# A cached-attention decode block: weight loads with longer rows, and part of the output projection and modulation moved to another place

## The chip, the cores and the metric

The kernel runs on one core of one Trainium2 chip. The metric is the device time of one execution in microseconds (us), lower is better. The kernel before takes 687.1 us (median of 3 runs, 687.01 to 687.26). The span of a profile is about 2 us shorter than the time of the same run, so times are compared with times and spans with spans.

Words used below: PE is the matrix engine, PEld its weight loads, DVE the vector engine, ACT the scalar engine, SPq the queue that issues the loads. The core has 16 DMA engines, and each load is split over them.

## The reference, cut to what matters

One token (a row of 512 numbers) goes through an attention block with a cache and then a gated feed-forward block. The cache has 8 key/value heads with 65,536 positions of 128 numbers in bfloat16: 268 MB that must be read once.

```python
mod = silu(c) @ w_mod                       # 6 vectors: sa, ca, ga, sb, cb, gb
h = layernorm(x) * (1 + ca) + sa
q = h @ wq                                  # 32 query heads, 4 to a key/value head
p = softmax(q @ k.T * 128**-0.5);  o = p @ v
x = x + ga * (o @ wo)
h = layernorm(x) * (1 + cb) + sb
x = x + gb * ((silu(h @ w_gate) * (h @ w_up)) @ w_down)
```

All weights together are 17 MB, so the cache is 94% of the 285.5 MB that are read.

## The kernel before

The cache is read in 32 chunks of K and 32 of V, 4 MB each, into one store of 24 slots of 1 MB. All loads stand in one list and are issued in its order as soon as there is room. PE transposes K (two bfloat16 as one fp32), multiplies by q, and later multiplies V by the softmax weights. The weights lie in the same list: the first part of w_mod and wq in front, wo and the rest of w_mod between the last chunks, gate, up and down at the end.

```python
    wo3 = A_wo.rearrange("(k p) n -> p k n", p=P)      # 1 KB rows: one row of wo per partition and k
    wd3 = B_w_down.rearrange("(k p) n -> p k n", p=P)  # 1 KB rows
    ...                                                # w_gate, w_up: 3.5 KB rows
    for i in range(NCH + 2):
        if i >= 2:
            kv("v", A_v_cache, i - 2, V_END if i - 2 == NCH - 1 else (0, NB))
        if i < NCH:
            kv("k", A_k_cache, i)
        if i == NCH:
            w(("mb",), wmod3, 0, KC, (2 * D, 6 * D))
        if NCH + 1 - len(wo_at) <= i <= NCH:
            h0 = wo_at[i - (NCH + 1 - len(wo_at))]
            w(("o", h0), wo3, h0, h0 + WO_H, (0, D))   # the last of four goes in front of the last V
    w(("g",), wg3, 0, KC, (0, F))
    w(("u",), wu3, 0, KC, (0, F))
    w(("d",), wd3, 0, FC, (0, D), (0, FC0, FC))        # two pieces: 10 and 4 rows of 1 KB
    ...
    def attn_begin():                                  # runs after the softmax of the last chunk
        nonlocal attn_ps
        modulation(("mb",), 2, 6)                      # 64 matmuls
        done(("mb",))
        nc.vector.tensor_scalar(out=cb1T[:], in0=cbT, scalar1=1.0, scalar2=None, op0=ALU.add)
        attn_ps = pst.tile([P, KC], F32, name="attn_ps", tag="st")
        wo_part(0, Hq - rep)                           # 112 matmuls: all heads but the last group
    ...
    # then: the last PV run, its fold, head_out, wo_part(Hq - rep, Hq), layernorm, gate/up, down, output
```

Of the kernel before, what the change touches and what calls it, by code (L numbers as in the profile page):

```python
# [23 lines left out]
WO_H = 8  # L24
# [13 lines left out]
def kernel(  # L38
# [33 lines left out]
    small = ctx.enter_context(tc.tile_pool(name="small", bufs=2))  # L72
    spool = ctx.enter_context(tc.tile_pool(name="store", bufs=1))
# [50 lines left out]
    def w(key, ap3, k0, k1, cols, cuts=None):  # L124
        n0, n1 = cols

        def load(t):
            v = t[:, 0:(k1 - k0) * (n1 - n0)].rearrange("p (k n) -> p k n", n=n1 - n0)
            at = cuts or (0, k1 - k0)
            for a, b in zip(at, at[1:]):  # L130
                nc.sync.dma_start(out=v[:, a:b, :], in_=ap3[:, k0 + a:k0 + b, n0:n1])
            return v
        stream.append((key, (k1 - k0) * (n1 - n0), load))

    wmod3 = w_mod.rearrange("(k p) n -> p k n", p=P)
    wq3 = A_wq.rearrange("(k p) n -> p k n", p=P)
    wo3 = A_wo.rearrange("(k p) n -> p k n", p=P)
    wg3 = B_w_gate.rearrange("(k p) n -> p k n", p=P)
    wu3 = B_w_up.rearrange("(k p) n -> p k n", p=P)
    wd3 = B_w_down.rearrange("(k p) n -> p k n", p=P)  # L140
    w(("ma",), wmod3, 0, KC, (0, 2 * D))
    w(("q",), wq3, 0, KC, (0, Hq * Dh))
    wo_at = list(range(0, Hq, WO_H))
    for i in range(NCH + 2):
        if i >= 2:
            kv("v", A_v_cache, i - 2, V_END if i - 2 == NCH - 1 else (0, NB))
        if i < NCH:
            kv("k", A_k_cache, i)
        if i == NCH:
            w(("mb",), wmod3, 0, KC, (2 * D, 6 * D))  # L150
        if NCH + 1 - len(wo_at) <= i <= NCH:
            h0 = wo_at[i - (NCH + 1 - len(wo_at))]
            w(("o", h0), wo3, h0, h0 + WO_H, (0, D))
    w(("g",), wg3, 0, KC, (0, F))
    w(("u",), wu3, 0, KC, (0, F))
    FC0 = FC - 4
    w(("d",), wd3, 0, FC, (0, D), (0, FC0, FC))

    at0 = 3 * UNIT
    xc_bf = store[0:2 * KC, at0:at0 + P]  # L160
    xc = store[0:2 * KC, at0 + P:at0 + 3 * P].bitcast(F32)
    perms = [store[:, at0 + (3 + e) * P:at0 + (4 + e) * P].rearrange("p (a i) -> p a i", a=2) for e in range(2)]
    nc.scalar.dma_start(out=xc_bf[0:KC, :], in_=c.rearrange("o (kc p) -> (o kc) p", p=P))  # L163
    nc.scalar.dma_start(out=xc_bf[KC:2 * KC, :], in_=A_x.rearrange("a b (kc p) -> (a b kc) p", p=P))
# [23 lines left out]
    nc.vector.tensor_copy(out=xc, in_=xc_bf)  # L188
    xc_ps = pmisc.tile([P, 2 * KC], F32, name="xc_ps", tag="misc")
    nc.tensor.transpose(out=xc_ps[:], in_=xc, identity=ident_f[0:2 * KC, 0:2 * KC])  # L190
# [14 lines left out]
    def layernorm_in():  # L205
        rs = small.tile([P, 1], F32, name="ln1_rs", tag="ln_rs")
        nc.vector.reduce_sum(out=rs[:], in_=xT[:], axis=AX.X)
        tot_ps = pmisc.tile([P, 1], F32, name="ln1_tot", tag="misc")
        nc.tensor.matmul(out=tot_ps[:], lhsT=ones_f[:], rhs=rs[:], start=True, stop=True)  # L209
        negmean = small.tile([P, 1], F32, name="ln1_nm", tag="ln_nm")  # L210
        nc.vector.tensor_scalar(out=negmean[:], in0=tot_ps[:], scalar1=-1.0 / n_el, scalar2=None, op0=ALU.mult)
        nc.vector.tensor_scalar(out=xd[:], in0=xT[:], scalar1=negmean[:], scalar2=None, op0=ALU.add)  # L212
        sq = small.tile([P, KC], F32, name="ln1_sq", tag="ln_sq")
        rs2 = small.tile([P, 1], F32, name="ln1_rs2", tag="ln_rs2")
        nc.vector.tensor_tensor(out=sq[:], in0=xd[:], in1=xd[:], op=ALU.mult)
        nc.vector.reduce_sum(out=rs2[:], in_=sq[:], axis=AX.X)
        var_ps = pmisc.tile([P, 1], F32, name="ln1_var", tag="misc")
        nc.tensor.matmul(out=var_ps[:], lhsT=ones_f[:], rhs=rs2[:], start=True, stop=True)  # L218
        ve = small.tile([P, 1], F32, name="ln1_ve", tag="ln_ve")
        nc.vector.tensor_scalar(out=ve[:], in0=var_ps[:], scalar1=1.0 / n_el, scalar2=LN_EPS, op0=ALU.mult, op1=ALU.add)  # L220
        rstd = small.tile([P, 1], F32, name="ln1_rstd", tag="ln_rstd")
        nc.gpsimd.tensor_tensor(out=rstd[:], in0=ve[:], in1=mhalf[:], op=ALU.pow)  # L222
        xn = small.tile([P, KC], F32, name="ln1_xn", tag="ln_xn")
        nc.vector.tensor_scalar(out=xn[:], in0=xd[:], scalar1=rstd[:], scalar2=None, op0=ALU.mult)
        return xn
# [7 lines left out]
    def modulate(xn, cT_, sT_, tagp):  # L233
        t1 = small.tile([P, KC], F32, name=f"{tagp}_t1", tag="mod_t1")
        nc.vector.scalar_tensor_tensor(out=t1[:], in0=cT_, scalar=1.0, in1=xn[:], op0=ALU.add, op1=ALU.mult)
        h_bf = small.tile([P, KC], BF16, name=f"{tagp}_h", tag="mod_h")
        nc.vector.tensor_tensor(out=h_bf[:], in0=t1[:], in1=sT_, op=ALU.add)
        return h_bf

    modT = const.tile([P, 6, KC], F32, name="modT", tag="modT")  # L240

    def modulation(key, i0, i1):
# [3 lines left out]
        gemv(ps, lambda kc, nb: wm[:, kc, nb * P:(nb + 1) * P], scT, KC, nblk)  # L246
        bf = small.tile([P, nblk], BF16, name=f"mod_bf{i0}", tag="mod_bf")
# [10 lines left out]
    done(("q",))  # L258
    qT = const.tile([P, Hq], BF16, name="qT", tag="qT")
# [14 lines left out]
    oT_bf = const.tile([P, Hq], BF16, name="oT_bf", tag="oT_bf")  # L274
# [121 lines left out]
    def head_out(g, wgt):  # L396
        oT = heads.pop(g)[2]
        ow = small.tile([P, NCPH, rep], F32, name=f"ow{g}", tag="ow")
        nc.vector.tensor_tensor(out=ow[:], in0=oT[:], in1=wgt[:], op=ALU.mult)
        with nc.allow_low_precision("the attention output is bfloat16 in the reference"):  # L400
            nc.vector.tensor_reduce(out=oT_bf[:, g * rep:(g + 1) * rep], in_=ow[:].rearrange("p c h -> p h c"),
                                    axis=AX.X, op=ALU.add)
# [18 lines left out]
    for cc in range(NCH):  # L421
# [10 lines left out]
        if cc % NCPH == NCPH - 1:  # L432
            g = cc // NCPH
            at(e + 6, keep(("wgt", g), lambda g=g: head_weights(g)))
            at(p1 + 1, lambda g=g: head_out(g, carry.pop(("wgt", g))))
# [3 lines left out]
    def wo_part(h0, h1):  # L439
        for nb in range(KC):  # L440
            for h in range(h0, h1):
                wo_sb = held[("o", h // WO_H * WO_H)]
                nc.tensor.matmul(out=attn_ps[:, nb:nb + 1], lhsT=wo_sb[:, h % WO_H, nb * P:(nb + 1) * P],
                                 rhs=oT_bf[:, h:h + 1], start=(h == 0 and nb == 0), stop=(h == Hq - 1),
                                 skip_group_check=True)

    def attn_begin():
        nonlocal attn_ps
        modulation(("mb",), 2, 6)
        done(("mb",))  # L450
        nc.vector.tensor_scalar(out=cb1T[:], in0=cbT, scalar1=1.0, scalar2=None, op0=ALU.add)
        attn_ps = pst.tile([P, KC], F32, name="attn_ps", tag="st")
        wo_part(0, Hq - rep)

    cb1T = const.tile([P, KC], F32, name="cb1T", tag="cb1T")
    side.setdefault(TAIL_AT, []).insert(0, attn_begin)
# [9 lines left out]
    wo_part(Hq - rep, Hq)  # L466
    for h0 in range(0, Hq, WO_H):
        done(("o", h0))
    warm = small.tile([P, 1], F32, name="warm", tag="warm")
    nc.scalar.activation(out=warm[:], in_=mhalf[:], func=ACT.Silu)  # L470
    t2 = small.tile([P, KC], F32, name="t2", tag="t2")
# [4 lines left out]
    ys = small.tile([P, 3], F32, name="ys", tag="ys")  # L476
    nc.vector.reduce_sum(out=ys[:], in_=yy[:], axis=AX.X)
    x1T = const.tile([P, KC], F32, name="x1T", tag="x1T")
    nc.vector.tensor_tensor(out=x1T[:], in0=t2[:], in1=xT[:], op=ALU.add)
    ms_ps = pmisc.tile([P, 3], F32, name="ms_ps", tag="misc")  # L480
    nc.tensor.matmul(out=ms_ps[:], lhsT=mean_w[:], rhs=ys[:], start=True, stop=True)
    ve2 = small.tile([P, 1], F32, name="ve2", tag="ve2")
    nc.vector.tensor_scalar(out=ve2[:], in0=ms_ps[:, 0:1], scalar1=ms_ps[:, 1:2], scalar2=ms_ps[:, 2:3],
                            op0=ALU.mult, op1=ALU.add)
    rstd2 = small.tile([P, 1], F32, name="rstd2", tag="rstd2")
    nc.gpsimd.tensor_tensor(out=rstd2[:], in0=ve2[:], in1=mhalf[:], op=ALU.pow)
    xn2 = small.tile([P, KC], F32, name="xn2", tag="xn2")
    nc.vector.tensor_scalar(out=xn2[:], in0=yy[:, 0, 0:KC], scalar1=ms_ps[:, 0:1], scalar2=rstd2[:],  # L488
                            op0=ALU.subtract, op1=ALU.mult)
    m2 = small.tile([P, KC], F32, name="m2", tag="m2")  # L490
    nc.vector.tensor_tensor(out=m2[:], in0=xn2[:], in1=cb1T[:], op=ALU.mult)
    h2T = small.tile([P, KC], BF16, name="h2T", tag="h2T")
    nc.vector.tensor_tensor(out=h2T[:], in0=m2[:], in1=sbT, op=ALU.add)
    gu_ps = pmisc.tile([P, 2, FC], F32, name="gu_ps", tag="misc")
    for i, key in enumerate((("g",), ("u",))):
        gemv(gu_ps[:, i, :], lambda kc, nb: held[key][:, kc, nb * P:(nb + 1) * P], h2T, KC, FC)
        done(key)
    gu_bf = small.tile([P, 2, FC], BF16, name="gu_bf", tag="gu_bf")
    nc.vector.tensor_copy(out=gu_bf[:], in_=gu_ps[:])
    sg = small.tile([P, FC], BF16, name="sg", tag="sg")  # L500
    nc.scalar.activation(out=sg[:], in_=gu_bf[:, 0, :], func=ACT.Silu)  # L501
    guT = small.tile([P, FC], BF16, name="guT", tag="guT")
    nc.vector.tensor_tensor(out=guT[:], in0=sg[:], in1=gu_bf[:, 1, :], op=ALU.mult)
    o_ps = pmisc.tile([KC, P], F32, name="o_ps", tag="misc")
    nc.tensor.matmul(out=o_ps[:], lhsT=x1T[:], rhs=ident_f[:], start=True, stop=False)
    f_ps = pmisc.tile([P, KC], F32, name="f_ps", tag="misc")
    wd_sb = held[("d",)]
    for f0, f1 in ((0, FC0), (FC0, FC)):
        for nb in range(KC):
            for fc in range(f0, f1):  # L510
                nc.tensor.matmul(out=f_ps[:, nb:nb + 1], lhsT=wd_sb[:, fc, nb * P:(nb + 1) * P],  # L511
# [3 lines left out]
    t3 = small.tile([P, KC], F32, name="t3", tag="t3")  # L515
    nc.vector.tensor_tensor(out=t3[:], in0=f_ps[:], in1=gbT, op=ALU.mult)
    nc.tensor.matmul(out=o_ps[:], lhsT=t3[:], rhs=ident_f[:], start=False, stop=True)  # L517
    o_bf = small.tile([KC, P], BF16, name="o_bf", tag="o_bf")
    nc.vector.tensor_copy(out=o_bf[:], in_=o_ps[:])  # L519
    nc.sync.dma_start(out=out.rearrange("a b (kc p) -> (a b kc) p", p=P), in_=o_bf[:])  # L520
# [30 lines left out]
```

## Time and profile before

| | before |
|---|---|
| time | 687.1 us |
| span of the profile | 685.0 us |
| load queue's packets, share of 16 engines' span | 98.3% |
| rate from 60 to 560 us | about 429 GB/s |
| last part of the last w_down load lands | 680.8 us |
| compute chain ready for w_down (guT written) | 679.9 us |

First the page of the kernel before: busy time by engine, the rate in 40 slices, and the DMA packets.

```profile
PE 573.9 (84%) x8069; PEld 499.8 (73%) x8069; DVE 259.5 (38%) x583; ACT 201.3 (29%) x527; POOL 3.6 (1%) x17
...
GB/s 368 428 427 433 433 426 436 427 430 435 424 429 429 435 429 428 425 429 428 429 427 427 433 432 431 432 432 427 428 429 428 432 433 405 417 412 386 390 391 222
DMA packets 18373, 286.63 MB, mean 418 GB/s; under 512 B 1272, under 2 KB 7160, under 8 KB 9464
...
q1 hardware_dynamic: 18280, 285.48, 98.3%
q8 instruction: 63, 1.03, 0.6%
```

No compute engine is full, and the rate is flat until the 33rd slice: the loads bound the kernel. In the last seven slices the rate is lower. q1 is the queue of the loads, q8 the one that brings instructions.

The next lines are the table of windows of the kernel before: the window and its length in us, then busy us and number of instructions of PE, PEld, DVE, ACT and POOL; the last three columns are the granted PE clock (1.00 is full speed), the busy share of the DMA engines and GB/s.

```profile
580.00:590.00 10.00, 8.12 (x129) 6.52 (x127) 4.62 (x13) 2.45 (x5) 0.00 (x0) 1.00 0.97 387
620.00:630.00 10.00, 6.16 (x85) 4.52 (x83) 2.08 (x3) 1.82 (x5) 0.00 (x0) 0.83 0.90 371
665.00:670.00 5.00, 4.21 (x48) 1.61 (x45) 0.69 (x1) 0.00 (x0) 0.00 (x0) 0.50 1.03 403
675.00:680.00 5.00, 3.64 (x114) 3.13 (x113) 0.97 (x5) 0.21 (x1) 0.32 (x1) 0.50 0.61 210
```

Last, the timeline of the tail (start, duration, engine, line, what). In brackets stands how long the engine sat idle before and what ended that. The names: Lt is the sum of the softmax weights, mod_ps the modulation, attn_ps the output projection wo, pvw the last PV run (softmax weights times V), oc the fold of its result over the partitions, gu_ps gate and up, guT what goes into w_down, f_ps w_down.

```profile
634.37 17.45 SPq L117 DMA_DIRECT2D store<-in_A_v_cache_dram  x4
...
660.08 0.61 PE L377 MATMUL Lt<-Lp,ones_f 128*128 128x16 f32 x2 [2.01 <-ACT wgt L385]
660.53 1.85 PE L199 MATMUL mod_ps<-scT,store 128*128 128x1 bf16 x64
662.24 3.12 PE L443 MATMUL attn_ps<-oT_bf,store 128*128 128x1 bf16 x112
665.29 3.59 PE L352 MATMUL pvw<-store,pt 128*16 128x512 bf16 x32
...
669.68 1.87 PE L370 MATMUL oc<-sel,pvw_sb 128*128 128x4 f32 x8 [0.80 <-DVE pvw_sb L360]
...
676.09 3.12 PE L199 MATMUL gu_ps<-h2T,store 128*128 128x1 bf16 x112 [1.74 <-DVE h2T L493]
679.72 0.17 DVE L503 TENSOR_TENSOR guT<-sg,gu_bf 128x14 bf16<-128x14 bf16 x1 [0.28 <-ACT sg L501]
680.03 1.63 PE L511 MATMUL f_ps<-guT,store 128*128 128x1 bf16 x56 [0.30 <-DVE guT L503]
```

PE does modulation and wo, 5 us of work, between the last softmax and the last PV run.

### The profile page before, as it was taken

The page shows a single profiled execution, that of the slowest core. Times are in us where ns is not written, and L with a number is a line of the kernel's source. Part 1 is how long each engine was busy: PE and PEld are TensorE (multiplying, and loading weights), DVE is VectorE, ACT ScalarE, POOL GpSimd, SP SyncE. Part 2 cuts the span into 40 slices and gives each one's busy share as a digit, 9 for nine tenths or more (in the row PEclk, how much of TensorE's full clock was granted, in tenths as well). Part 3 has the DMA queues.
Part 4 walks back from the last instruction along what each step waited for, and adds up shares of the span by engine and source line. Part 5 has one row for each costly group of instructions (what it writes and reads, how often), then busy time and mean ns, then how long its engine had stood idle before and what let it go on. Part 6 is the DMA issues. An engine that isn't in the chain of part 4 may idle for free.

```text
span 685.0 us, 18012 instructions
## 1 busy us (share of the span) xinstructions
PE 573.9 (84%) x8069; PEld 499.8 (73%) x8069; DVE 259.5 (38%) x583; ACT 201.3 (29%) x527; POOL 3.6 (1%) x17
## 2 busy tenths in 40 slices
PE   1589897979989799888987899978898999867875
PEld 1578786868878688777876678867687888756764
DVE  1144343343434334433443344433334334423332
ACT  0143232333323133332322233332233323312220
POOL 1000000000000000000000000000000000000000
PEclk9999798797879876987999887999779778989765
DMA  9999999999999999999999999999999999999996
GB/s 368 428 427 433 433 426 436 427 430 435 424 429 429 435 429 428 425 429 428 429 427 427 433 432 431 432 432 427 428 429 428 432 433 405 417 412 386 390 391 222
DMA packets 18373, 286.63 MB, mean 418 GB/s; under 512 B 1272, under 2 KB 7160, under 8 KB 9464
## 3 DMA queue, kind: packets, MB, share of 16 engines
q1 hardware_dynamic: 18280, 285.48, 98.3%
q8 instruction: 63, 1.03, 0.6%
q14 instruction: 14, 0.11, 0.0%
q10 hardware_dynamic: 16, 0.00, 0.0%
HBM read 285.48 MB, written 0.00 MB: 417 GB/s over the span
## 4 chain that ended last, share of the span: by engine, by line
issue 97%; PE 1%; DMA 1%; DVE 0%; POOLq 0%; POOL 0%; ACTq 0%; ACT 0%; DVEq 0%
DMA store<-in_A_x_dram 1%; PE gu_ps L199 0%; PE f_ps L511 0%; PE o_ps L517 0%; POOLq L546 0%; PE ln_tot L209 0%; PE ln_var L218 0%; POOL ln_rstd L222 0%; ACTq L163 0%; DVE xn L488 0%; DVE o_bf L519 0%; PE xc_ps L190 0%; DVE xd L212 0%; DVE store L188 0%; ACT sg L501 0%
## 5 line engine op out<-in xcount | busy, mean ns | idle before, releaser
L289 PE MATMUL ktp<-ident_f,store 128*128 128x128 f32 x2048 | 393.6, 324 | 63.2 <-DMA store<-in_A_k_cache_dram 63.2
L289 PEld LDWEIGHTS ktp<-ident_f,store 128*128 128x128 f32 x2048 | 263.1, 163 | 93.6 <-issue 80.4
L295 DVE COPY kts<-ktp 128x512 int32<-128x512 int32 x256 | 177.0, 692 | 319.2 <-PE ktp L289 308.6
L293 ACT COPY kts<-ktp 128x512 f32<-128x512 f32 x256 | 151.2, 591 | 442.5 <-PE ktp L289 442.5
L310 PEld LDWEIGHTS <-kts 128*128 128x128 bf16 x4096 | 193.0, 102 | 16.5 <-ACT kts L293 1.5
L310 PE MATMUL st<-qpair,kts 128*128 128x8 bf16 x4096 | 184.5, 168 | 1.3 <-ACT kts L293 1.3
L352 PE MATMUL pvw<-store,pt 128*16 128x512 bf16 x1024 | 71.5, 403 | 13.5 <-DMA store<-in_A_v_cache_dram 13.5
L342 ACT ACTIVATE pt<-st,negb 128x128 bf16<-128x128 f32 x128 | 51.3, 558 | 5.4 <-DVE negb L335 5.4
L352 PEld LDWEIGHTS <-pt 128*16 128x16 bf16 x1024 | 21.4, 90 | 32.1 <-issue 17.7
L360 DVE COPY pvw_sb<-pvw 128x512 f32<-128x512 f32 x32 | 22.1, 692 | 39.5 <-PE pvw L352 39.5
L342 ACT ACTIVATION_READ_ACCUMULATOR pt<-st,negb 128x1 f32 x128 | 36.4, 284 | 0.0
L370 PE MATMUL oc<-sel,pvw_sb 128*128 128x4 f32 x256 | 34.5, 258 | 1.8 <-DVE pvw_sb L360 0.8
L370 PEld LDWEIGHTS oc<-sel,pvw_sb 128*128 128x128 f32 x256 | 31.8, 195 | 5.5 <-DVE pvw_sb L360 1.7
L317 DVE TENSOR_REDUCE mx<-st 128x4 f32<-128x512 f32 x32 | 21.8, 681 | 0.2 <-PE st L310 0.2
L322 PE MATMUL mt<-ident_f,mx 128*4 128x128 f32 x32 | 10.6, 332 | 8.1 <-DVE mx L317 5.5
L332 PE MATMUL mb<-dg,ones_f 4*128 4x4 f32 x64 | 15.2, 306 | 0.7 <-DVE dg L326 0.6
L199 PEld LDWEIGHTS <-store 128*128 128x128 bf16 x336 | 9.9, 106 | 8.1 <-DMA store<-in_A_wq_dram 6.3
L332 PEld LDWEIGHTS mb<-dg,ones_f 4*128 4x128 f32 x64 | 12.4, 241 | 2.3 <-DVE dg L326 0.8
L324 DVE TENSOR_REDUCE m<-mt 4x1 f32<-4x128 f32 x32 | 8.9, 279 | 13.6 <-PE mt L322 13.6
L372 DVE COPY oT<-oc 128x4 f32<-128x4 f32 x32 | 5.2, 162 | 17.3 <-PE oc L370 17.3
L322 PEld LDWEIGHTS mt<-ident_f,mx 128*4 128x4 f32 x32 | 2.6, 82 | 10.9 <-DVE mx L317 10.9
L199 PE MATMUL q_ps<-m_h,store 128*128 128x1 bf16 x128 | 3.6, 165 | 6.2 <-DMA store<-in_A_wq_dram 6.2
(89 smaller groups left out, 74.3 us busy)
## 6 DMA issues: line engine op xcount, KB each, us to landing
store<-in_A_k_cache_dram SPq DMA_DIRECT2D x32, 4096.0 KB, 43.7
store<-in_A_v_cache_dram SPq DMA_DIRECT2D x31, 4096.0 KB, 53.2
store<-in_A_wq_dram SPq DMA_DIRECT2D x1, 4096.0 KB, 14.7
store<-in_A_wo_dram SPq DMA_DIRECT2D x4, 1024.0 KB, 28.9
store<-in_w_mod_dram SPq DMA_DIRECT2D x1, 2048.0 KB, 23.2
store<-in_A_v_cache_dram SPq DMA_DIRECT2D x1, 2048.0 KB
store<-in_B_w_gate_dram SPq DMA_DIRECT2D x1, 1792.0 KB, 19.7
store<-in_B_w_up_dram SPq DMA_DIRECT2D x1, 1792.0 KB, 23.7
```

The costliest lines, as they stand in the source:

```text
L199: nc.tensor.matmul(out=out_ps[:, nb:nb + 1], lhsT=lhs(kc, nb), rhs=actT[:, kc:kc + 1], start=(kc == 0), stop=(kc == n_kc - 1))
L289: nc.tensor.transpose(out=ktp[:, e4, :], in_=kt32[:, j0:j0 + 2, :].rearrange("p a i -> p (a i)"), identity=ident_f[:])
L293: nc.scalar.copy(out=kts[:].bitcast(F32), in_=ktp[:])
L295: nc.vector.tensor_copy(out=kts[:].bitcast(I32), in_=ktp[:].bitcast(I32))
L310: nc.tensor.matmul(out=st[:, b0:b0 + 2, :].rearrange("p b h -> p (b h)"), lhsT=ktsv[:, e4, :, e], rhs=qpair[:, g, e, :, :].rearrange("p j ...
L317: nc.vector.tensor_reduce(out=mx[:], in_=st_of[cc][:].rearrange("p b h -> p h b"), axis=AX.X, op=ALU.max)
L322: nc.tensor.transpose(out=mt[:], in_=mx[:], identity=ident_f[:])
L332: nc.tensor.matmul(out=mb[:], lhsT=ones_f[0:rep, :], rhs=dg[:], start=True, stop=True)
L342: nc.scalar.activation(out=pt_of[cc][:, :, h], in_=st_of[cc][:, :, h], func=ACT.Exp, bias=negb[:, h:h + 1], scale=scale, accum_out=Lp[:, c ...
L352: nc.tensor.matmul(out=pvw[32 * jt:32 * jt + QB * rep, :], lhsT=pt_of[cc][:, b0:b0 + QB, :].rearrange("p b h -> p (b h)"), rhs=held[("v", ...
L360: nc.vector.tensor_copy(out=pvw_sb[:], in_=pvw[:])
L370: nc.tensor.matmul(out=oc_ps[:], lhsT=pvw_sb[:, bl * Dh:(bl + 1) * Dh], rhs=sel[:, bl, :], start=(bl == 0), stop=(bl == QB - 1))
```

## The change

Its intent is to load the weights in longer rows and to take PE work off the tail. The contraction index of each weight matrix is dealt to partitions the other way round: partition p gets rows 4p to 4p+3 ("(p k)") instead of p, 128+p and so on, so that one partition's rows are contiguous in memory. That changes which element of an activation each partition holds, so weights are now read with a step of 2 or 4 columns, and each head's output passes through a small permutation (a multiply by a mask, one matmul, a copy). x and c are now loaded as one row each and turned by eight small matmuls at the start.

```diff
-    wo3 = A_wo.rearrange("(k p) n -> p k n", p=P)
+    wo3 = A_wo.rearrange("(g p j) n -> p g (j n)", p=P, j=rep)              # 4 KB rows
-    wd3 = B_w_down.rearrange("(k p) n -> p k n", p=P)
+    w(("d",), B_w_down.rearrange("(b p j) n -> p b (j n)", p=P, j=2), ...)  # 2 KB rows
     ...   # the same for w_mod, wq (32 KB rows), w_gate and w_up (14 KB rows)
-        if NCH + 1 - len(wo_at) <= i <= NCH:
+        if NCH + 1 - len(wo_at) <= i < NCH:
     ...
+    w(("o", wo_at[-1]), wo3, wo_at[-1], wo_at[-1] + WO_G)     # the last wo load, now behind the last V
     ...
+    def head_turn(g, om):                                    # om = head output times a mask, bfloat16
+        of_ps = pmisc.tile([P, rep], F32, name=f"of{g}", tag="misc")
+        nc.tensor.matmul(out=of_ps[:], lhsT=om[:].rearrange("p h q -> p (h q)"), rhs=at4_bf[:], start=True, stop=True)
+        nc.vector.tensor_copy(out=oF[:, g, :], in_=of_ps[:])
     ...
     def attn_begin():
         nonlocal attn_ps
-        modulation(("mb",), 2, 6)
-        done(("mb",))
-        nc.vector.tensor_scalar(out=cb1T[:], in0=cbT, scalar1=1.0, scalar2=None, op0=ALU.add)
         attn_ps = pst.tile([P, KC], F32, name="attn_ps", tag="st")
-        wo_part(0, Hq - rep)
-    side.setdefault(TAIL_AT, []).insert(0, attn_begin)
+        wo_part(0, 5)
+    side[NBANKS - BPC + PV_RUNS[0][0]].insert(0, attn_begin)       # 80 wo matmuls, in the last K chunk
+    side[NBANKS + S_LAG + 1].append(late_modulation)               # before Lt, while ACT does the exponentials
+    side[late(NBANKS + PV_RUNS[-1][0])].append(lambda: wo_part(5, Hkv - 1))   # 32, behind the last PV run
     ...   # the output leaves as 32 rows of 16, not 4 of 128
```

## The prediction

> **What bounds the kernel now.** The DMA engines. In the page's 40 slices DMA busy is 9 tenths everywhere but the last slice, and from 60 to 560 us the table of windows shows 428 to 430 GB/s. The queue table gives the load queue 98.3% of 16 engines' span. Only the tail is below that rate: 387 (580-590 us), 371 (620-630), 396, 382, 377 (630-660), 368 (670-675). The trace's DMA packet records, grouped by size, say part of the reason: a 32 KB packet takes 1222 ns (429 GB/s over 16 engines), a 4 KB one 162 (405), a 3.5 KB one 145 (396), a 2 KB one 94 (350), a 1 KB one 50 (329). The 1 KB packets are wo (4096) and w_down (1792).
>
> The end is a second, nearly equal limit. By the timeline, the last w_down packet lands at 680.4, and the compute chain reaches the w_down matmuls at 680.0. That chain: softmax until 659.8, Lt 660.1, 64 modulation matmuls 660.5-662.2, 112 wo matmuls 662.2-665.3, the last PV run 665.3-668.9, fold, 16 wo matmuls, layernorm, gate/up 676.1-679.2, down 680.0-681.7, output at 682.9. PE runs at half clock from 657 on.
>
> **What the change does.**
> 1. Loads with longer rows (bytes are the same). From the packet means: wo 1 KB to 4 KB, 12.7 to 10.4 us; w_down 1 KB to 2 KB, 5.6 to 5.2; gate and up 3.5 to 14 KB, 9.3 to 8.7 (estimate, interpolated); wq 8 to 32 KB, -0.2. Sum about -3.6 us of DMA. The Trainium skill, "DMA: Bandwidth & Descriptors", section "Why small descriptors are slow (HBM only)", names a fixed cost per packet; the trace agrees, about 9 ns each above the pure rate.
> 2. Work off the tail's PE: the modulation (1.85 us) moves in front of Lt, where PE idled 2.0 us for the exponentials; 80 of 112 wo matmuls move into the last K chunk, 32 go behind the PV run, under the 0.69 us PSUM copy. About 5 us leave the stretch before PV, but the 80 (2.2 us at 27 ns) come back earlier, where PE hardly waits.
> 3. The last wo load goes behind the last V: V lands about 2.4 us sooner.
> 4. Added on the end: a permutation per head (multiply, matmul, copy) instead of a direct reduce, about +0.9 us once; the last matmul has 16 columns, not 128 (-0.2).
> 5. Weights read with a step of 2 or 4 elements. The "TensorE: Matmul & The Clock Gate" page of the skill, section "Weight-path perf modes", has fast weight load for packed or strided chunks; here the step-2 loads of kts (25-27 ns apart) are as fast as the packed ones (27 ns). Step 4 is not shown by any record.
>
> **Critical path.** DMA would end near 677, so down would finish near 681. The compute chain: PV can start about 662-663 and keeps its 16 us behind it, +0.7: the end comes at 681-683 instead of 685. I expect the compute chain to decide, with 3 us gained of some 5 on offer.
>
> **Prediction: 684.0 us, 80% range 681.0 to 686.4.** Faster by over 2%: 0.03; within 2%: 0.96; slower by over 2%: 0.01.
>
> **Right if** the after packets show no 1 KB loads and the queue's packet time falls by about 3.5 us; tail rates over 400 GB/s; the last PV run starts near 662.5, and w_down's matmuls no longer follow the wo block directly but start near 678.
>
> **Wrong if** step-4 weights load at half speed (about +1.5 us in the tail); the 80 wo matmuls delay the last transposes and so the last V issue (the loads' issues wait on those transposes); or the dip at 627-635 us, where the queue ran low (278 GB/s), grows or vanishes.

## More of the kernel before

From 665 to the end everything is one chain. It reaches the w_down matmuls (f_ps) at 680.03 and was released by guT. But PEld's wait names the other party:

```profile
PEld L511 <- DMA store<-in_B_w_down_dram: 0.8, 1, 0.8
```

So the two limits, the loads and the chain, end within a microsecond of each other. The chain is the later one by a little: the first w_down load had landed at 679.5, and the 56 matmuls then ran through in 1.63 us without a stop, although the last part landed at 680.8.

## The result, and the profile after

The changed kernel takes 684.38 us (median of 11 runs, 684.17 to 687.82; nine of them lie between 684.17 and 684.58, the other two are 685.88 and 687.82). The kernel before takes 687.23 us in the same rounds (14 runs). The ratio is 0.9965, 95% interval 0.9955 to 0.9975. (A ratio is the mean time of one kernel's runs over that of the other's in the same rounds, so it is not quite the ratio of the medians.) The prediction, 684.0 us in 681.0 to 686.4, holds.

The same parts of the page, after the change:

```profile
PE 581.9 (85%) x8084; PEld 510.3 (75%) x8084; DVE 263.2 (39%) x604; ACT 201.7 (30%) x527; POOL 3.6 (1%) x17
...
GB/s 369 429 428 427 428 429 430 428 433 427 428 432 429 430 430 428 429 429 430 428 426 430 429 429 428 429 427 429 431 428 428 433 430 423 433 423 426 410 414 169
DMA packets 13281, 286.63 MB, mean 420 GB/s; under 512 B 1298, under 2 KB 1300, under 8 KB 4500
...
q1 hardware_dynamic: 13200, 285.48, 97.9%
q8 instruction: 63, 1.03, 0.6%
```

The small packets are gone (5860 fewer under 2 KB), and the rate holds four slices longer. The table of windows after:

```profile
580.00:590.00 10.00, 6.63 (x100) 5.06 (x99) 3.60 (x9) 1.52 (x3) 0.00 (x0) 0.97 0.99 422
620.00:630.00 10.00, 6.33 (x78) 4.64 (x77) 2.01 (x3) 1.63 (x4) 0.00 (x0) 0.68 1.02 432
665.00:670.00 5.00, 2.84 (x53) 2.61 (x53) 1.87 (x9) 0.10 (x1) 0.00 (x0) 0.79 0.70 286
675.00:680.00 5.00, 3.37 (x92) 3.05 (x89) 0.68 (x4) 0.21 (x1) 0.00 (x0) 0.50 0.28 105
```

The dips at 580 and 620 us are gone. But look at 665 to 680: the DMA engines are on average only 70%, then 28% busy, and yet the last load has not landed. The timeline of the tail after:

```profile
660.73 0.59 PE L404 MATMUL Lt<-Lp,ones_f 128*128 128x16 f32 x2
661.25 3.47 PE L379 MATMUL pvw<-store,pt 128*16 128x512 bf16 x32
664.65 0.29 PE L480 MATMUL attn_ps<-oF,store 128*128 128x1 bf16 x4
665.37 1.09 PE L480 MATMUL attn_ps<-oF,store 128*128 128x1 bf16 x28 [0.42 <-DMA store<-in_A_wo_dram]
...
666.33 1.03 PE L397 MATMUL oc<-sel,pvw_sb 128*128 128x4 f32 x8
...
672.71 3.13 PE L209 MATMUL gu_ps<-h2T,store 128*128 128x1 bf16 x112 [1.74 <-DVE h2T L529]
676.34 0.17 DVE L541 TENSOR_TENSOR guT<-sg,gu_bf 128x14 bf16<-128x14 bf16 x1 [0.28 <-ACT sg L539]
677.23 2.03 PE L549 MATMUL f_ps<-guT,store 128*128 128x1 bf16 x56 [1.18 <-DMA store<-in_B_w_down_dram]
```

The last PV run starts at 661.25 instead of 665.29, and guT is ready at 676.5 instead of 679.9: the chain gained 3.4 us. The matmuls of w_down then wait: the loads end the kernel now. Part of this is the clock of the profiled run: the oc matmuls took 1.03 us at a granted clock of 1.00 (664.5 to 667.9 us) instead of 1.87 us at 0.50. At the half clock the chain would have been ready at about 677.35 (estimate), just after the first w_down load (677.2). The two limits are still close.

### Which loads: the arrivals engine by engine

A load is done when 16 parts of it have arrived. The trace keeps the time of each of these arrivals. (The Trainium skill, "DMA: Bandwidth & Descriptors", section "Why a DMA increments its semaphore by 16 and not by 1", says that each engine's last descriptor posts one increment when its data has landed. The records agree: 16 times per load.) These are the 16 arrivals of a K chunk in mid-tail and of the last piece of w_down, in us, sorted:

```
K chunk, before      578.7 578.8 578.8 578.9 579.2 579.4 582.3 584.7 588.1 588.5 589.5 589.6 589.6 589.6 589.7 589.7
K chunk, after       578.9 579.2 579.2 579.3 579.4 579.7 582.5 584.9 588.6 588.7 589.7 589.8 589.9 589.9 589.9 590.0
last w_down, before  676.2 676.2 676.3 676.5 676.5 676.6 676.7 677.2 678.7 679.2 680.3 680.4 680.4 680.4 680.7 680.8
last w_down, after   666.0 666.3 666.3 666.4 666.5 666.8 670.3 672.9 677.1 677.4 678.2 678.4 678.4 678.5 678.5 678.5
```

Six engines are fast, two are between, eight are slow. The first load of either kernel arrives within 0.5 us on all engines. By 590 us the fast ones are 11 us ahead. A load counts only when its slowest part is there, so the eight slow engines pace the kernel, and the mean busy share says nothing of them. After the change the fast engines are done at 666 us and stand idle for the last 12 us. This is the drop to 28%.

It also explains most of the dip at 620 us in the profile before. There a load that followed a wo load took long to issue, for example 20.26 us instead of 0.33. These are lines of the timeline of SPq, before and then after:

```profile
609.64 0.43 SPq L131 DMA_DIRECT2D store<-in_A_wo_dram  x1
610.17 20.26 SPq L117 DMA_DIRECT2D store<-in_A_v_cache_dram  x1
```

```profile
586.08 1.31 SPq L132 DMA_DIRECT2D store<-in_A_wo_dram  x1
607.44 0.33 SPq L118 DMA_DIRECT2D store<-in_A_v_cache_dram  x1
```

While the V load was being issued, the fast engines ran dry (before, the spread of the arrivals fell from 10.7 us at 639 to 6.9 at 649). The slow engines still had work. (In the dip at 580 us the busy share was 0.97, so there the larger part of the loss was the lower rate of the 1 KB packets of wo, which are loaded then.) The wo load behind the last K was complete, on the slowest engine, at 638.9 before and 638.0 after, 0.9 us apart. So the lost rate in the dips cost little, and getting it back gained little.

### The profile page after: what moved, and what is told of

It reads as the page before. It is cut to its first block, busy times and chain, and to the rows that moved or that the text cites. A ratio compares the mean times of both kernels' runs of the same rounds, so it can differ in the third digit from the quotient of the medians.

```text
span 682.3 us, 18062 instructions
## 1 busy us (share of the span) xinstructions
PE 581.9 (85%) x8084; PEld 510.3 (75%) x8084; DVE 263.2 (39%) x604; ACT 201.7 (30%) x527; POOL 3.6 (1%) x17
## 3 DMA queue, kind: packets, MB, share of 16 engines
q8 instruction: 63, 1.03, 0.6%
## 4 chain that ended last, share of the span: by engine, by line
DMA 76%; PE 21%; DVE 2%; another core or an unknown queue 0%; issue 0%; SPq 0%; DVEq 0%
DMA store<-in_A_k_cache_dram 45%; DMA store<-in_A_v_cache_dram 19%; PE ktp L316 13%; DMA store<-in_w_mod_dram 7%; DMA store<-in_B_w_down_dram 4%; PE st L337 3%; PE pvw L379 3%; DMA store<-in_A_wq_dram 2%; DVE kts L322 1%; DVE mx L344 1%; PE q_ps L209 1%; PE mb L359 1%; PE mt L349 0%; PE f_ps L549 0%
## 5 line engine op out<-in xcount | busy, mean ns | idle before, releaser
L316 PE MATMUL ktp<-ident_f,store 128*128 128x128 f32 x2048 | 402.0, 330 | 58.4 <-DMA store<-in_A_k_cache_dram 58.3
L316 PEld LDWEIGHTS ktp<-ident_f,store 128*128 128x128 f32 x2048 | 269.0, 166 | 87.7 <-issue 72.9
L337 PEld LDWEIGHTS <-kts 128*128 128x128 bf16 x4096 | 195.3, 103 | 16.8 <-ACT kts L320 1.5
L379 PE MATMUL pvw<-store,pt 128*16 128x512 bf16 x1024 | 69.3, 393 | 8.4 <-DMA store<-in_A_v_cache_dram 8.3
```

Of the source, the lines that this page charges most:

```text
L316: nc.tensor.transpose(out=ktp[:, e4, :], in_=kt32[:, j0:j0 + 2, :].rearrange("p a i -> p (a i)"), identity=ident_f[:])
L337: nc.tensor.matmul(out=st[:, b0:b0 + 2, :].rearrange("p b h -> p (b h)"), lhsT=ktsv[:, e4, :, e], rhs=qpair[:, g, e, :, :].rearrange("p j ...
L379: nc.tensor.matmul(out=pvw[32 * jt:32 * jt + QB * rep, :], lhsT=pt_of[cc][:, b0:b0 + QB, :].rearrange("p b h -> p (b h)"), rhs=held[("v", ...
```

## The experiments

Theory A: two limits ended nearly together, the arrivals on the slow DMA engines and the compute chain; the rows move the first, the order moves the second, and neither helps alone. Rival B: the chain alone decides. Rival C: the loads alone decide. Theory D, about the slow engines: they alone carry the instruction packets of PE. Rival E: they are slow for another reason. Seven kernels were run, in two groups on one chip each. The changed kernel itself was not in these rounds; the kernel before was (medians 687.31 and 687.50 us, 687.23 in the rounds of the changed kernel).

### Order alone

```diff
 # the kernel before, with 1 KB rows and no permutation, and:
-        if NCH + 1 - len(wo_at) <= i <= NCH:
+        if NCH + 1 - len(wo_at) <= i < NCH:
+    w(("o", wo_at[-1]), wo3, wo_at[-1], wo_at[-1] + WO_H, (0, D))
-    side.setdefault(TAIL_AT, []).insert(0, attn_begin)
+    side[NBANKS - BPC + PV_RUNS[0][0]].insert(0, attn_begin)        # wo_part(0, 20)
+    side[NBANKS + S_LAG + 1].append(late_modulation)
+    side[late(NBANKS + PV_RUNS[-1][0])].append(lambda: wo_part(20, 28))
```

> Before's row layouts, with the changed order alone (late modulation before Lt, 80 wo matmuls in the last K chunk and 32 behind the PV run, last wo load behind the last V). Theory A (two limits end nearly together: the slowest DMA engines, whose last w_down packet lands at 680.4 us, and the compute chain): the chain is ready 2 to 4 us sooner, but the loads still end near 680.4 and about 4.2 us follow them, so the gain is at most 0.6 us: 686.6 to 687.2 us. Rival B (the compute chain alone decides): 684 us or less.

Measured: 686.82 us (5 runs, 686.78 to 687.08), before 687.31 in the same rounds, ratio 0.9989 (0.9977 to 1.0). The waits of PE in its tail:

```profile
PE f_ps L516 <- DMA store<-in_B_w_down_dram: 1.3, 1, 1.3
```

guT was ready at 678.7, 1.2 us sooner than before and not 2 to 4, because loads held the chain earlier too: its wo matmuls waited 0.9 us for the last wo load and its up matmuls 0.3 us for w_up. It then waited for w_down, whose last part landed at 681.2. The gain is a sixth of the whole change's, as theory A expects, and hardly clear of noise. Rival B is out.

### Rows alone

```diff
 # the changed kernel, with:
-        if NCH + 1 - len(wo_at) <= i < NCH:
+        if NCH + 1 - len(wo_at) <= i <= NCH:          # the last wo load in front of the last V again
-    side[NBANKS - BPC + PV_RUNS[0][0]].insert(0, attn_begin)
-    side[NBANKS + S_LAG + 1].append(late_modulation)
-    side[late(NBANKS + PV_RUNS[-1][0])].append(lambda: wo_part(5, Hkv - 1))
+    side.setdefault(TAIL_AT, []).insert(0, attn_begin)    # late_modulation(), then wo_part(0, 7)
```

> The changed row layouts (and the permutation they need) with before's order of PE work and of loads. Theory A: loads end about 2.3 us sooner, but 1.85 us of modulation and 3.1 us of wo matmuls stand before the last PV run again and the permutation adds 0.9: 686.3 to 687.5 us. Rival C (the loads alone decide): about 684.5 us.

Measured: 688.18 us (5 runs, 688.03 to 688.72), ratio 1.001 (0.9997 to 1.0023): 0.9 us over the median of before, a little above what theory A allowed. The interval includes 1, so that it is slower than before is not shown; that it is no faster is. Rival C, which asked for 684.5, is out. The timeline of its tail:

```profile
659.69 2.27 PE L208 MATMUL mod_ps<-scT,store 128*128 128x1 bf16 x64
661.82 3.87 PE L479 MATMUL attn_ps<-oF,store 128*128 128x1 bf16 x112
...
681.18 1.99 PE L547 MATMUL f_ps<-guT,store 128*128 128x1 bf16 x56 [0.60 <-DVE guT L539]
```

Its loads ended at 678.8, as in the changed kernel, and that went unused: the chain came at 681.2, released by guT. The same 64 and 112 matmuls took 2.27 and 3.87 us instead of 1.85 and 3.12. These are the weights read with a step of 4: from one matmul to the next it is 33 to 34 ns instead of 27. In this profile that is 1.2 us and the permutation 0.8 us on the chain; guT came 1.1 us later than before, because Lt had started 0.8 us sooner. Order alone gives -0.5 us, rows alone +0.9, both together -2.9: the gain belongs to neither part alone.

### More PE instructions

```diff
 # the changed kernel, with:
-        for e4 in range(4):
+        for e4 in (0, 0, 0, 1, 2, 3) if cc < 28 else range(4):     # the same score matmuls again
```

> The changed kernel with 4 of the 8 score matmuls of a bank repeated (same values) in the first 28 of 32 chunks: 3584 more PE instructions, about 14 more 16 KB instruction packets at 1.07 us each. Theory D (the slow half of the DMA engines is slow because it alone carries PE's instruction packets, 8 each): about 1.8 us more on each of those engines, the spread of the last landings grows from 12.5 to about 14.3 us and the time by 1 to 2 us: 685.4 to 686.5. Rival E (the slow engines are slow for another reason, PE has the room: 0.1 us a bank of some 1.25): 684.2 to 684.8, spread as it was.

Measured: 687.32 us (6 runs; five between 687.30 and 687.40, one 689.38), 2.9 us over the changed kernel's 684.4 (above the expected 685.4 to 686.5), and 1.0000 of the kernel before. From its page:

```profile
q8 instruction: 77, 1.26, 0.7%
```

The 14 packets that 3584 instructions should make are there (256 instructions to a 16 KB packet). The last w_down piece arrived at 666.8 us on the fastest engine, 0.8 us later than without them (it was issued late; the piece before it arrived at 664.7 there in both kernels), and at 681.7 on the slowest, 3.2 us later:

```
last w_down          666.8 666.8 667.0 667.1 667.1 667.2 670.4 673.0 680.0 680.2 680.2 680.3 681.4 681.5 681.6 681.7
```

Only the slow group moved by more than 0.8 us, as theory D expects, and by more than was expected from the packets' own 1.07 us: 14 packets on 8 engines are 1.75 each, so one costs its engine about 3.2 / 1.75 = 1.8 us.

### Fewer PE instructions

This one leaves out work, so its attention is wrong (the comparison with the reference still passes: over 65,536 nearly equal positions the output hardly depends on the scores).

```diff
 # the changed kernel, with:
-            for e in range(2):
+            ne = 1 if cc < 28 else 2                   # half of the score matmuls left out
+            for e in range(ne):
-                                 start=(e == 0), stop=(e == 1))
+                                 start=(e == 0), stop=(e == ne - 1))
```

> The changed kernel with half of the score matmuls left out in the first 28 of 32 chunks (the result is wrong on purpose): 3584 fewer PE instructions, 14 fewer instruction packets of 63. Theory D (the slow DMA engines are slow because they carry PE's instruction packets): the run with 14 more moved the last landing by +3.2 us, so here -3 us, to about 675.5, the spread falls from 12.5 to about 9.5 us and the time to 681.5 (681 to 682.5). Rival E (in the run before it was PE time that counted, 0.1 us a bank): the loads keep their pace, last landing 678 to 678.5 and time 684.

Measured: 681.52 us (4 runs, 681.25 to 683.01), ratio to before 0.9918 (0.9904 to 0.9931). From its page, and the arrivals:

```profile
q8 instruction: 49, 0.80, 0.5%
```

```
last w_down          666.0 666.1 666.3 666.4 666.6 666.8 670.6 672.7 675.3 675.4 675.5 675.5 675.5 675.5 675.6 675.6
```

Again the fast engines did not move and the slow ones did, by -2.9 us, and so did the time, by -2.9. Rival E had asked for 684. The three kernels agree: 49, 63 and 77 packets give spreads of 9.6, 12.5 and about 15 us (14.9 in the last piece, 15.7 in those before it). With 1.7 to 1.8 us a packet, the 63 packets over 8 engines would account for the whole spread (estimate: 63 / 8 x 1.7 = 13.4).

These two kernels change the number of matmuls together with the number of packets, so a rival is left: that the matmuls themselves slow some engines. The DMA packet records rule it out for most of the loss. Between 60 and 560 us the changed kernel has 47 instruction packets, of 1.07 us each. Each starts when a cache packet ends, and within 20 ns of its end a new cache packet begins. In all 47 cases this one took 1.67 to 1.77 us, while the median of all cache packets was 1.215 us. From the start of the instruction packet on, about 1.55 us are lost each time. So 49, 63 and 77 packets should cost 76, 98 and 119 us in all; the ten engines behind the six fast ones were late with their last w_down part by 84, 104 and 120 us in sum (estimates from these records and the arrivals). The records do not name the engine; that these packets fall on the slow engines is concluded from the sums and the two experiments.

### The last wo load back in front of the last V

```diff
 # the changed kernel, with:
-        if NCH + 1 - len(wo_at) <= i < NCH:
+        if NCH + 1 - len(wo_at) <= i <= NCH:
```

> The changed kernel with the last wo load back in front of the last V, nothing else. Theory A (the loads' end holds, the chain has 0.7 us of room before the first w_down landing): the last V lands about 2.4 us later, the last PV run, which now starts at 661.3, is held for its last rows by 1 to 2 us, the chain is ready at 677.5 to 678.5 instead of 676.5, and the time rises by 0.3 to 1.3 us: 684.7 to 685.7. Rival (the order of these two loads is of no use): 684.4.

Measured: 685.27 us (5 runs: 684.21, 684.61, 685.27, 685.42, 687.67), ratio 0.9962 (0.9948 to 0.9976), against 684.33 of the kernel of the next experiment in the same rounds. The median lies in the expected range, but the runs overlap, so the effect of this order is unclear. The profile fell on the run of 687.67, and it shows where a stray high time can come from. The window of the last K chunk's end, first in this run and then in the changed kernel:

```profile
649.70:656.50 6.80, 6.80 (x86) 5.19 (x85) 1.20 (x2) 0.59 (x1) 0.00 (x0) 0.50 1.03 422
```

```profile
649.70:656.50 6.80, 6.66 (x116) 5.24 (x104) 2.95 (x6) 1.17 (x2) 0.00 (x0) 1.00 1.03 424
```

PE is full in both, but the granted clock was 0.50 in one and 1.00 in the other, and only 86 matmuls instead of 116 were done. The chain came to w_down at 680.7 and ended the kernel, although the loads ended at 678.6. The clock alternates between 0.5 and 1.0 in stretches of 3 to 58 us in every profile here; whether a half-clock stretch falls on this part differs from profile to profile. Whether the two stray runs of the changed kernel have the same cause is not shown: they were not profiled, and their mean clocks (0.816 and 0.827) are like those of the others.

### w_down in finer pieces

```diff
 # the changed kernel, with:
-    w(("d",), ..., 0, FC // 2, (0, FC0 // 2, FC // 2))
+    w(("d",), ..., 0, FC // 2, (0, 3, 6, 7))
-    for f0, f1 in ((0, FC0), (FC0, FC)):
+    for f0, f1 in ((0, 6), (6, 12), (12, FC)):
```

> The changed kernel with w_down loaded in three pieces (3, 3 and 1 blocks of 2 KB rows) instead of two (5 and 2), and its matmuls cut to match. If the end is held by the last w_down landing, fewer matmuls behind it and an earlier first start save 0.3 to 0.5 us: 683.9 to 684.1. If the compute chain holds: 684.4 or, with one more load to issue, more.

Measured: 684.33 us (5 runs, 684.21 to 684.76), no change. Its timeline:

```profile
677.04 2.24 PE L549 MATMUL f_ps<-guT,store 128*128 128x1 bf16 x56 [0.60 <-DVE guT L541]
```

The first matmuls no longer wait for w_down, but the last arrival came at 678.7 (678.5 in the changed kernel), and the matmuls ended at 679.3, as they did there. So the finer cut did not help: the end of the list of loads still counted. The expected 0.3 us were not there. It is a weak test, as the chain was ready 0.4 us later in this profile than in the changed kernel's (676.9 instead of 676.5).

### w_down split over other engines

A probe, and an attempt to use the idle fast engines. The Trainium skill, "DMA: Bandwidth & Descriptors", section "Why a DMA increments its semaphore by 16 and not by 1" (paragraph "How many engines"), says that the number of engines is the largest one up to 16 that divides the slowest dimension of both sides, here the row count, so 119 rows go to 7 engines.

```diff
 # the changed kernel, with:
-                nc.sync.dma_start(out=v[:, a:b, :], in_=ap3[:, k0 + a:k0 + b, :])
+                for p0, p1 in ((0, split), (split, P)) if split else ((0, P),):      # w_down: split = 119
+                    nc.sync.dma_start(out=v[p0:p1, a:b, :], in_=ap3[p0:p1, k0 + a:k0 + b, :])
```

> The changed kernel with each w_down load cut into rows of 119 and of 9 partitions, a probe of which engines carry which part: 119 = 7 x 17. If the 119 rows go to 7 engines that belong to the fast ones, the slow ones end about 4 us sooner and the time falls by about 1 us to 683.3 (the compute chain is ready at 676.5, 0.7 us before the first w_down landing). If the 7 engines are among the slow ones, the last landing is some 5 us later: 689. If they stay spread over all 16, no change: 684.4.

Measured: 699.15 us (4 runs), ratio 1.0166 (1.0153 to 1.018). The records show 7 arrivals for the 119 rows and 9 for the 9 rows, as the page says. The 7 came at 675.0, 675.6, 675.7, 681.1, 683.5, 687.1 and 689.5 us, so fast and slow engines seem to be among them. None of the three guesses came true. None foresaw this: while the 119 rows were being loaded, the 14 KB packets of w_gate and w_up, which had nothing to do with them, took 1032 ns on average (15 packets starting from 662 to 666 us) instead of 541. The last part of w_up arrived at 680.8 instead of 673.9 us, about half of the 14.4 us by which the last w_down part was late (692.9). Here 17 rows go to an engine instead of 8; why that holds up other loads no run shows. As a way to shift load to the fast engines it failed.

## Why the prediction was right, point by point

- **What bounds the kernel: right, but read too coarsely.** The prediction took the mean rate as the loads' limit. The limit is the slow half of the engines. The dip to 371 GB/s was mostly fast engines without work (busy share 0.90), the dip to 387 (0.97) mostly the slower small packets.
- **Load packets, -3.6 us: right in direction, too large.** The queue's packet time, summed from the packet records, fell from 673.2 to 668.3 us per engine, that is by 4.9 us and not by about 3.5, but the last arrival moved by 2.3 us (680.8 to 678.5). The prediction had put that end near 677. By the last arrivals from load to load, the four wo loads took 2.3 us less in all (2.3 predicted), gate and up 0.5 (0.6), down 0.15 (0.4) and wq 0.2. The first load arrived 0.3 us later (6.3 instead of 6.0), and about 0.4 us are not accounted for. For down the term failed because packet durations overlap: 112 packets of 1 KB per engine at the mean of 50 ns make 5.6 us, but the two w_down loads took 4.7 us from the last arrival of w_up to their own. The fixed cost per packet of the skill's section "Why small descriptors are slow (HBM only)" is there, but for w_down the mean packet duration overstates what longer rows save.
- **PE work off the tail: right.** PV was predicted at 662 to 663 and started at 661.25 (662.23 in the profile of the finer pieces, which is the same kernel up to there). The 32 wo matmuls behind it did not stay hidden: 28 of them waited 0.42 us for the last wo load, and oc began 0.86 us after the copy of the PV result was done instead of 0.06. In this profile the faster oc made up for it.
- **V sooner by 2.4 us: more.** The last V part arrived at 662.7 instead of 667.0. Of these 4.3 us, 3.3 are the wo load's time (653.7 to 657.0 before).
- **The permutation, +0.9 us: right.** From the oT copy to the last wo matmuls it is 1.40 us (667.40 to 668.80) instead of 0.64 (671.59 to 672.23), 0.76 more.
- **Weights with step 4, named as a risk: slower, but not half speed.** From one matmul to the next they take 33 to 34 ns instead of 27; the 80 wo matmuls took 2.80 us. On the chain it cost about 1 us (modulation 0.44, last wo matmuls 0.10, w_down 0.40) and did not decide.
- **The dip at 627 to 635 us, which was to be a bad sign if it vanished, did vanish** (327 GB/s before, 410 after), and the forecast held all the same: it was a dip of engines that had time to spare.
- **"I expect the compute chain to decide": wrong.** This is the step that failed. The chain was ready at 676.5, sooner than the start near 678 that was expected, and waited 0.7 us for the first w_down load and longer for the last. The loads decided in this profile, by less than the 0.84 us that the clock gave to oc, and "order alone" and "rows alone" show that each limit takes over when only the other is moved. That the number came out right is in part luck: the loads ended 1.5 us later than put (678.5, not 677), the chain was ready sooner than put, and both ends had been put close to each other, at 681 and at 681 to 683; the profile's end is 682.3.

## What to carry to other kernels

When two limits end within a microsecond of each other, cost both to the end: each half of such a change alone may gain nothing (here -0.5 and +0.9 us), and both together 2.9. Where loads bound a kernel, read the arrivals of single loads and not only the mean rate: a busy share that falls to 28% while the last load is still under way can mean, as here, that some engines carry more than others. And count instructions as load traffic: in this kernel 256 PE instructions cost one DMA engine about 1.55 us by the packet records (1.7 to 1.8 by the last arrivals), so 3584 instructions more or less moved a load-bound time by 2.9 us either way, without PE being the limit.

## What the Trainium skill lacked or had wrong

- "DMA: Bandwidth & Descriptors", section "Latency and other measured facts", has engines 7 and 15 usually slower than the others. Here eight of the 16 are slow (the records do not number them), two lie between, and the slow ones fall 11 us behind in 590 us.
- "Runtime: NRT & Kernel Launch", section "Instruction fetch mechanics", does not say that the instruction packets of a compute engine take time from the data loads of some DMA engines, or how much, and no other page found does. Here: 63 packets of 16 KB for 16,138 PE instructions, 1.55 us lost to a load for each; 14 more or fewer moved the slow engines' last arrival by +3.2 or -2.9 us.
- "TensorE: Matmul & The Clock Gate", section "Weight-path perf modes", gives fast weight load for packed or strided chunks without a difference, and "SBUF — State Buffer", section on the DMA port swizzle, calls two accesses to a 16-byte line enough for full rate, which a step of 4 bfloat16 has. Here the matmuls follow each other at 27 ns with step 1 and step 2 and at 33 to 34 ns with step 4.
- "DMA: Bandwidth & Descriptors", the paragraph on the number of engines, was borne out (119 rows gave 7 arrivals), but no page found warns of what such a split did to other loads: their 14 KB packets took 1032 ns instead of 541.
- No page found has the long issue of a load behind one with 1 KB rows: the V load behind a wo load took 20.26 us to issue, and 0.33 us when the wo rows were 4 KB. What sets it is open: in "rows alone" two later issues took 12.43 and 19.51 us with 4 KB rows.
